# One part of a float64-to-float32 weight conversion: an activation on ScalarE in place of a shift on VectorE

## The chip, the cores and the metric

The kernel runs on one core of a Trainium2 chip. A core has a matrix engine (TensorE, PE in the profile, with its weight loads as PEld), VectorE (DVE), ScalarE (ACT), GpSimd (POOL), and SyncE (SP), which here issues most of the transfers. Each engine works through its own queue in order and waits for the others only through semaphores. The metric is the device time of one execution in microseconds (us); lower is better.

## The reference

Three layers follow one another. All inputs are made in float32 or float64; the weights reach the kernel as float64.

```python
# attention, batch 8, heads 8, 576 positions, head width 64, 32 packing rows p
p_packed = softmax(p @ k.T / 8) @ v          # per head
x = softmax(q @ p_packed.T / 8) @ p_packed   # -> 4608 tokens x 512
# first layer
h = ((x @ w1) * (x @ w2)) @ w3               # 512 -> 1024 -> 1024
x = h @ w_out                                # 1024 -> 512
# second layer, h -> 0 below -1, h above 1, (h + 1)**2 / 4 between
g = gate(x @ w_in)                           # 512 -> 2048
out = g @ w_out2                             # 2048 -> 512
```

## The kernel before

The weights are float64 in memory, eight bytes a value, and the engines work on four. `as_float32` (lines 113 to 138) turns a raw tile of 128 x 512 float64 values into float32 by bits. It views a value as four 16-bit quarters (quarter 0 the lowest). `scale` (L124, ScalarE) reads the upper 32 bits as a float, multiplies by 2^-112 and writes the tile `cvt`. `parts` writes two halves of the output: L129 (VectorE) takes quarter 1 shifted right by 13 bits, so its top three bits, into the low half, and L131 (VectorE) takes the sign bit of quarter 3 into the high half. `join` (L135, VectorE) shifts `cvt` left by three bits and ORs it into the output. There are 72 such conversions.

Forty of them are in the first stage. `ORDER` is a written list of 40 raw tiles: 'o' is a tile of the first layer's w_out (its float32 tile is called `wo`), '3' one of w3 (`w3f`), '12' one of w1 or w2 (`w`). The loop at line 534 goes through this list. In step i it emits the matrix work of `STEPS[i]`, then `convert_begin(i + 1)` (L124 of the next tile), then `convert_end(i)`: L129 and L131 of tile i, L135 of tile i-1, and the load of tile i+4 into the raw buffer that tile i frees (`RAW` is 4 buffers, L110, issued by SP). Only then come the vector and scalar parts of the attention steps. The matrix engine uses the tiles in two ways: L494 multiplies w3 by w_out, one step of four products for each '3' tile, and L192 multiplies w1 and w2 by the packed attention rows.

The other 32 conversions prepare the second layer's weights. `weight_tasks` (line 584) makes eight groups of 18 small tasks, and the loop at line 703 puts one task behind each unit of the first layer's work for batches 1 to 6. Four tasks of a group are conversions (`convert`, L610), into tiles named `cvx`; the others split or combine them (`hl`, L633 on ScalarE and L634 on VectorE) and store them (L641, issued from ScalarE's queue). Here one conversion has its three functions called in a row, there is one `cvt` buffer, and three raw buffers. Between the tasks stand the units: `ab_unit` (products L386, then L396 on ScalarE and L398 on VectorE, then a split L103/L104), `x2_unit` (products L410, then L437 on ScalarE and a store), and the attention of the next batch, with its two exponentials (L215 and L300), its maximum (L208), its score transposes (L294) and its packed rows `pp` (L265).

From about 515 us on the second layer runs without conversions.

Of the kernel before, what the change touches and what calls it, by code (L numbers as in the profile page):

```python
# [13 lines left out]
AF = mybir.ActivationFunctionType  # L14
ALU = mybir.AluOpType
# [40 lines left out]
def fused_kernel(ctx: ExitStack, tc, qT, kT, vv, pb, w1, w2, w3T, wo, win, wout, out):  # L56
    nc = tc.nc
# [55 lines left out]
    def as_float32(pool, raw, out, bufs=1):  # L113

        if raw.dtype == F32:
            return lambda: None, lambda: None, lambda: nc.vector.tensor_copy(out=out, in_=raw)
        quarters = raw.bitcast(U16).rearrange("p (n four) -> p n four", four=4)
        t = pool.tile([P, 512], F32, name="cvt", tag="cvt", bufs=bufs)  # L120
        halves = out.bitcast(U16).rearrange("p (n two) -> p n two", two=2)

        def scale():
            nc.scalar.activation(  # L124
                out=t, in_=raw.bitcast(F32).rearrange("p (n two) -> p n two", two=2)[:, :, 1],
                func=AF.Copy, scale=2.0 ** -112)

        def parts():
            nc.vector.tensor_scalar(  # L129
                out=halves[:, :, 0], in0=quarters[:, :, 1], scalar1=13, scalar2=None, op0=ALU.logical_shift_right)  # L130
            nc.vector.tensor_scalar(  # L131
                out=halves[:, :, 1], in0=quarters[:, :, 3], scalar1=0x8000, scalar2=None, op0=ALU.bitwise_and)

        def join():
            nc.vector.scalar_tensor_tensor(  # L135
                out=out.bitcast(I32), in0=t.bitcast(I32), scalar=3, in1=out.bitcast(I32),
                op0=ALU.logical_shift_left, op1=ALU.bitwise_or)
        return scale, parts, join
# [1035 lines left out]
```

## Time and profile before

| | |
|---|---|
| device time, median of 3 runs | 1330.1 us (1329.04 to 1331.21) |
| profiled execution, its own time | 1334.05 us |
| its span in the profile | 1332.1 us |
| PE busy | 1270.8 us (95% of the span) |
| DVE busy | 879.0 us (66%), 1462 instructions |
| ACT busy | 678.3 us (51%), 1144 instructions |
| L124 on ScalarE | 72 instructions |
| L129 on VectorE | 72 instructions in four groups (32, 16, 16 and 8) |

All durations are from the one profiled execution. Busy time is a union of intervals on an engine, so an idle gap on PE is time in which it had nothing to run. A row of a timeline gives the start, the duration, the engine, the line and operation, and in brackets the idle time just before and who ended it. A duration reaches from start to end; instructions of one engine overlap a little, so the distance between two starts is shorter than a duration. Idle time of an engine that nothing waits for costs nothing.

### The profile page before, as it was taken

How to read it: one execution, taken by the hardware profiler on the slowest of the kernel's cores; microseconds unless marked ns; L12 is line 12 of the kernel's file. 1: busy time of each engine (PE TensorE's matmuls, PEld its weight loads, DVE VectorE, ACT ScalarE, POOL GpSimd, SP SyncE). 2: the span in 40 equal slices, each digit the busy share in tenths (PEclk: the TensorE clock that was granted, in tenths of full speed). 3: DMA queues.
4: the chain of work that ended last, by engine and by line, in shares of the span. 5: the costliest groups of instructions: out<-in, count | busy, mean ns of one | idle time of the engine just before them, and what ended most of it. 6: DMA issues, size and time to landing. Idle time of an engine off the chain costs nothing.

```text
span 1332.1 us, 21124 instructions
## 1 busy us (share of the span) xinstructions
PE 1270.8 (95%) x8184; PEld 1061.1 (80%) x8184; DVE 879.0 (66%) x1462; ACT 678.3 (51%) x1144; POOL 0.7 (0%) x6
## 2 busy tenths in 40 slices
PE   6989889999999999999999999998899899999998
PEld 2367778889888989998777877787878688888888
DVE  5874777778677779635787877877555546455464
ACT  4444354545444555535667766766554343434433
POOL 0000000000000000000000000000000000000000
PEclk9999999999999999999999999999999999999999
DMA  9771575547375543358667675766999967768665
GB/s 362 238 243 59 194 223 180 199 175 273 133 244 155 218 178 125 134 215 299 233 218 270 213 283 199 250 224 205 320 373 375 366 223 266 249 230 290 212 221 176
DMA packets 121299, 307.82 MB, mean 231 GB/s; under 512 B 10352, under 2 KB 45168, under 8 KB 116720
## 3 DMA queue, kind: packets, MB, share of 16 engines
q1 hardware_dynamic: 84304, 237.14, 50.8%
q10 hardware_dynamic: 36896, 69.35, 15.1%
q8 instruction: 64, 1.05, 0.3%
q14 instruction: 35, 0.29, 0.1%
HBM read 200.41 MB, written 106.04 MB: 230 GB/s over the span
## 4 chain that ended last, share of the span: by engine, by line
PE 62%; DMA 15%; DVE 13%; ACT 6%; issue 3%; ACTq 1%; SPq 0%; DVEq 0%
PE x L1090 13%; PE psk L410 13%; PE psk L386 10%; DMA g<-L 7%; PE x L810 7%; PE z L1090 7%; PE y L1090 4%; PE z L810 3%; DMA wi<-hl 2%; PE y L810 2%; PE psk L192 1%; DVE x2s L681 1%; DVE L L874 1%; DMA raw<-w3T 1%; ACT r L818 1%
## 5 line engine op out<-in xcount | busy, mean ns | idle before, releaser
L386 PE MATMUL psk<-at,m 128*128 128x288 f32 x1494 | 215.6, 300 | 4.1 <-DVE at L327 1.9
L386 PEld LDWEIGHTS psk<-at,m 128*128 128x128 f32 x1494 | 201.9, 189 | 18.7 <-issue 11.7
L410 PEld LDWEIGHTS psk<-g,w 128*128 128x128 f32 x1500 | 200.1, 189 | 18.8 <-ACT st L437 7.8
L410 PE MATMUL psk<-g,w 128*128 128x288 f32 x1500 | 206.4, 297 | 4.8 <-ACT st L437 3.3
L810 PE MATMUL x<-x2s,wi 128*128 128x512 f32 (+1 forms) x720 | 163.0, 370 | 3.0 <-ACT m L881 3.0
L956 DVE TENSOR_TENSOR op<-raw,op 128x1024 fp32r<-128x1024 f32 (+1 forms) x94 | 101.7, 1114 | 78.5 <-ACT op L955 78.3
L810 PEld LDWEIGHTS x<-x2s,wi 128*128 128x128 f32 x720 | 126.1, 188 | 28.2 <-ACT m L881 4.5
L955 ACT ACTIVATE op<-raw 128x1024 fp32r<-128x1024 f32 (+1 forms) x94 | 87.3, 967 | 86.0 <-DVE raw L947 38.1
L1090 PE MATMUL x<-op,w 128*128 128x512 f32 (+1 forms) x480 | 103.6, 374 | 4.9 <-DVE op L956 3.2
L1090 PEld LDWEIGHTS x<-op,w 128*128 128x128 f32 x480 | 84.7, 191 | 23.0 <-DVE op L956 5.0
L1090 PE MATMUL x<-op,hwi 128*128 128x512 f32 (+1 forms) x480 | 100.4, 368 | 0.0
L1090 PEld LDWEIGHTS x<-op,hwi 128*128 128x128 f32 x480 | 83.1, 188 | 15.8
L398 DVE TENSOR_TENSOR tb<-psk,ta 128x288 f32<-128x288 f32 x124 | 56.3, 454 | 37.1 <-ACT ta L396 19.5
L821 ACT ACTIVATE r<-r 128x1024 f32<-128x1024 f32 (+1 forms) x80 | 78.0, 975 | 2.5
L956 DVE TENSOR_TENSOR op<-r,op 128x1024 fp32r<-128x1024 f32 (+1 forms) x46 | 50.2, 1118 | 43.5 <-ACT op L955 43.4
L494 PE MATMUL psk<-wo,w3f 128*128 128x512 f32 x128 | 61.4, 631 | 11.9 <-DVE w3f L135 11.9
L634 DVE TENSOR_TENSOR hl<-cvx,hl 128x512 fp32r<-128x512 f32 x56 | 38.4, 686 | 47.0 <-ACT hl L633 44.5
L810 PE MATMUL x<-x2s,ws 128*128 128x512 f32 (+1 forms) x240 | 59.6, 382 | 10.2 <-DVE L L885 9.1
L124 ACT ACTIVATE cvt<-raw 128x512 f32<-128x512 f32 x72 | 48.3, 676 | 40.0 <-DMA raw<-w3T 9.8
L881 ACT ACTIVATE m<-x 128x512 f32<-128x512 f32 (+1 forms) x40 | 22.1, 552 | 90.2 <-PE x L810 81.2
L955 ACT ACTIVATE op<-r 128x1024 fp32r<-128x1024 f32 (+1 forms) x46 | 43.2, 970 | 41.7 <-DVE r L947 14.9
L396 ACT ACTIVATE ta<-psk 128x288 f32<-128x288 f32 x125 | 50.2, 402 | 25.6 <-PE psk L386 21.2
(111 smaller groups left out, 1899.5 us busy)
## 6 DMA issues: line engine op xcount, KB each, us to landing
raw<-g SPq DMA_DIRECT2D x86, 512.0 KB, 5.0
g<-L SPq DMA_DIRECT2D x32, 1024.0 KB, 6.5
r<-g SPq DMA_DIRECT2D x42, 512.0 KB, 5.4
ws<-ws ACTq DMA_DIRECT2D x38, 512.0 KB, 4.9
g<-U SPq DMA_DIRECT2D x64, 256.0 KB, 6.3
w<-hl ACTq DMA_DIRECT2D x28, 512.0 KB, 3.1
x2d<-st ACTq DMA_DIRECT2D x72, 144.0 KB, 2.3
v<-vv SPq DMA_DIRECT2D x8, 1280.0 KB, 7.5
```

Source lines behind the costliest of these rows:

```text
L124: nc.scalar.activation(out=t, in_=raw.bitcast(F32).rearrange("p (n two) -> p n two", two=2)[:, :, 1], func=AF.Copy, scale=2.0 ** -112)
L386: nc.tensor.matmul(ps[w][:, :HS], m_tile[b, w, n][:, s, G, c0 * P:(c0 + 1) * P], at_tile[b][:, G, v, hf * HS:(hf + 1) * HS], start=(k == 0 ...
L396: nc.scalar.activation(out=bs, in_=ps[1][:, :HS], func=AF.Copy)
L398: nc.vector.tensor_tensor(out=g, in0=ps[0][:, :HS], in1=bs, op=ALU.mult)
L410: nc.tensor.matmul(ps, w34[kt][:, s, mt * P:(mt + 1) * P], g_t[kt, hf][:, v, :], start=(kt == kts[0] and n == 0), stop=(kt == kts[-1] and ...
L494: nc.tensor.matmul(acc[4 * hf + m], w3f[hf, j][:, m * P:(m + 1) * P], wof[j], start=(j == 0), stop=(j == 7))
L634: nc.vector.tensor_tensor(out=lo, in0=q[a], in1=hi.bitcast(F32), op=ALU.subtract)
L810: nc.tensor.matmul(bank[s, b][:, :N], w, x2_t[t, q][:, m, k, :N], start=(j == 0 and q in (A11, S1, A12)), stop=(j == 5), skip_group_check= ...
L821: nc.scalar.activation(out=r, in_=r, func=AF.Square)
L955: nc.scalar.activation(out=o[:, :, 0, :N], in_=a[0], func=AF.Copy)
L956: nc.vector.tensor_tensor(out=o[:, :, 1, :N], in0=a[0], in1=o[:, :, 0, :N].bitcast(F32), op=ALU.subtract)
L1090: nc.tensor.matmul(bank[b][d][:, :N], w2_t[q][j // 2][:, 2 * (j % 2) + k, s, d * P:(d + 1) * P], op[x][:, k, v, :N], start=start and k == ...
```

## The change

The low half of the output, the top three bits of quarter 1, is made by ScalarE: the 16-bit integer is multiplied by 2^-13, 4095.5/8192 is taken off, and the result is rounded to a 16-bit integer, which gives the same whole number as the shift. The VectorE shift goes away. It stands in the same place in the program, so it falls into ScalarE's queue there.

```diff
         def parts():
-            nc.vector.tensor_scalar(
-                out=halves[:, :, 0], in0=quarters[:, :, 1], scalar1=13, scalar2=None, op0=ALU.logical_shift_right)
+            nc.scalar.activation(
+                out=halves[:, :, 0], in_=quarters[:, :, 1], func=AF.Copy, scale=2.0 ** -13, bias=-4095.5 / 8192)
             nc.vector.tensor_scalar(
                 out=halves[:, :, 1], in0=quarters[:, :, 3], scalar1=0x8000, scalar2=None, op0=ALU.bitwise_and)
```

In the first stage the ScalarE queue before begins with the scalings of seven tiles one after another, up to the first exponential (`raw` is the float64 tile, `cvt` the scaled one):

```order
L124 ACT_TABLE_LOAD
L124 ACTIVATE cvt<-raw 128x512 x7
L215 ACTIVATE big,sum<-psm,nb 128x576
L124 ACTIVATE cvt<-raw 128x512 x2
L215 ACTIVATE big,sum<-psm,nb 128x576
```

The same place now:

```order
L124 ACT_TABLE_LOAD
L124 ACTIVATE cvt<-raw 128x512 x2
L129 ACTIVATE wo_140<-raw 128x512
L124 ACTIVATE cvt<-raw 128x512
L129 ACTIVATE w3f<-raw 128x512
L124 ACTIVATE cvt<-raw 128x512
L129 ACTIVATE wo_150<-raw 128x512
L124 ACTIVATE cvt<-raw 128x512
L129 ACTIVATE wo_158<-raw 128x512
L124 ACTIVATE cvt<-raw 128x512
L129 ACTIVATE wo_174<-raw 128x512
```

The low half of tile i (the first L129 is that of tile 0) stands behind the scaling of tile i+1, which waits for tile i+1 to be loaded.

In the first group of the second layer's weights, VectorE's queue before, around the second conversion (`mx` and `nb` feed the exponential, `tb` and `g` are the first layer's):

```order
L208 TENSOR_REDUCE mx<-psm 128x1
L210 TENSOR_SCALAR nb<-mx 128x1
L129 TENSOR_SCALAR cvx<-raw 128x512
L131 TENSOR_SCALAR cvx<-raw 128x512
L135 SCALAR_TENSOR_TENSOR cvx<-cvt,cvx 128x512
L398 TENSOR_TENSOR tb<-psk_1626,ta 128x288
```

ScalarE's queue now, at the third conversion of the same group, with the exponential ahead of it and `ta`, which L398 needs, behind it:

```order
L215 ACTIVATE big,sum<-psm,nb 128x576
L124 ACTIVATE cvt<-raw 128x512
L129 ACTIVATE cvx<-raw 128x512
L396 ACTIVATE ta<-psk_1685 128x288
L103 ACTIVATE g_1663<-tb 128x288
```

VectorE loses the row L129 there and the rest keeps its order; ScalarE has one instruction more between the scaling and `ta`.

## Rows read from the trace of the kernel before

**Rows 1.** The page's first part: engine, busy us (share of span), instructions.
```profile
PE 1270.8 (95%) x8184; PEld 1061.1 (80%) x8184; DVE 879.0 (66%) x1462; ACT 678.3 (51%) x1144; POOL 0.7 (0%) x6
```

**Rows 2.** Stretches: length, busy PE, PEld, DVE, ACT, POOL, clock, DMA share, GB/s.
```profile
45.00:77.00 32.00, 27.42 (x110) 11.35 (x108) 30.33 (x62) 15.28 (x27) 0.00 (x0) 1.00 0.64 221
164.00:200.00 36.00, 30.98 (x307) 27.59 (x304) 25.95 (x60) 19.25 (x47) 0.00 (x0) 0.95 0.69 213
200.00:515.00 315.00, 307.98 (x2900) 275.96 (x2899) 234.72 (x486) 160.14 (x363) 0.00 (x0) 1.00 0.55 192
```

**Rows 3.** Groups by line and shape: busy us, mean ns of one, idle before.
```profile
L124 ACT ACTIVATE cvt<-raw 128x512 f32<-128x512 f32 x72 | 48.3, 676 | 40.0 <-DMA raw<-w3T 9.8 <-DMA raw<-wo 8.5 <-DMA raw<-w 8.2
...
L633 ACT ACTIVATE hl<-cvx 128x512 fp32r<-128x512 f32 x56 | 35.3, 630 | 32.8 <-DMA wi<-hl 12.7 <-DVE cvx L135 7.4 <-ACT st L437 5.2
...
L955 ACT ACTIVATE op<-raw 128x1024 fp32r<-128x1024 f32 x75 | 76.2, 1054 | 75.2 <-DVE raw L947 33.8 <-DVE L L1067 25.7 <-DMA raw<-g 10.4
...
L881 ACT ACTIVATE m<-z 128x512 f32<-128x512 f32 x32 | 18.5, 579 | 0.8 <-PE z L810 0.8
...
L129 DVE TENSOR_SCALAR cvx<-raw 128x512 uint16<-128x512 uint16 x32 | 14.7, 458 | 0.0
```

**Rows 4.** Timeline of PE, first 100 us, where it sat idle.
```profile
18.01 1.19 PE L181 MATMUL psm<-qk,pb 128*64 128x288 f32 x8 [2.44 <-ACT big L215]
...
46.49 7.33 PE L494 MATMUL psk<-wo,w3f 128*128 128x512 f32 x16 [1.48 <-DVE w3f L135]
...
59.27 1.13 PE L494 MATMUL psk<-wo,w3f 128*128 128x512 f32 x2 [1.19 <-DVE w3f L135]
...
74.39 1.60 PE L386 MATMUL psk<-at,m 128*128 128x288 f32 x9 [1.50 <-DVE m L104]
...
97.22 2.89 PE L386 MATMUL psm<-at,m 128*128 128x288 f32 x12 [4.00 <-ACT st L437]
```

**Rows 5.** Timeline of ACT and DVE in the first 30 us.
```profile
26.36 1.26 ACT L124 ACTIVATE cvt<-raw 128x512 f32<-128x512 f32 x2
...
13.87 0.44 DVE L131 TENSOR_SCALAR wo<-raw 128x512 uint16<-128x512 uint16 x1
14.20 0.68 DVE L135 SCALAR_TENSOR_TENSOR wo<-cvt,wo 128x512 int32<-128x512 int32 x1
14.80 0.47 DVE L129 TENSOR_SCALAR w3f<-raw 128x512 uint16<-128x512 uint16 x1
15.15 0.46 DVE L131 TENSOR_SCALAR w3f<-raw 128x512 uint16<-128x512 uint16 x1
```

**Rows 6.** Raw tiles: load times of L110 to 115 us, then when tiles are taken up.
```profile
DMA to landing us min/median/max: 3.5/5.3/10.2
...
36.83 0.68 ACT L124 ACTIVATE cvt<-raw 128x512 f32<-128x512 f32 x1 [0.89 <-DMA raw<-w]
...
45.07 0.47 DVE L129 TENSOR_SCALAR w3f<-raw 128x512 uint16<-128x512 uint16 x1 [1.07 <-DMA raw<-w3T]
...
45.13 0.69 ACT L124 ACTIVATE cvt<-raw 128x512 f32<-128x512 f32 x1 [1.75 <-DMA raw<-w3T]
```

**Rows 7.** Waits of the whole run: us in total, times, longest.
```profile
DVE cvx L135 <- ACT cvt L124: 12.4, 10, 2.1
```

**Rows 8.** Timeline of ACT, DVE and PE, 366 to 389 us, rows that wait.
```profile
367.10 0.66 ACT L124 ACTIVATE cvt<-raw 128x512 f32<-128x512 f32 x1
...
367.79 0.69 DVE L135 SCALAR_TENSOR_TENSOR cvx<-cvt,cvx 128x512 int32<-128x512 int32 x1 [0.80 <-ACT cvt L124]
...
375.34 0.63 ACT L633 ACTIVATE hl<-cvx 128x512 fp32r<-128x512 f32 x1 [2.11 <-DMA wi<-hl]
...
379.02 0.34 PE L274 MATMUL psm<-ident,pp 128*128 128x128 f32 x1 [0.52 <-DVE pp L265]
...
388.61 0.72 PE L192 MATMUL psm<-qk,ppt 64*32 64x288 f32 x16 [2.02 <-DVE big L294]
```

**Rows 9.** Timeline of PE and DVE at two other groups of conversions.
```profile
277.16 0.69 DVE L135 SCALAR_TENSOR_TENSOR cvx<-cvt,cvx 128x512 int32<-128x512 int32 x1
278.87 1.32 PE L410 MATMUL psk<-g,w 128*128 128x288 f32 x8 [1.36 <-ACT st L437]
...
409.85 3.44 PE L410 MATMUL psk<-g,w 128*128 128x288 f32 x24 [0.51 <-ACT st L437]
```

## The prediction

> **What bounds the kernel now.** The page's first part comes first: the matrix engine is busy for 1270.8 of 1332.1 us [rows 1], so all that any change elsewhere can win is the 61.3 us in which it sits idle. VectorE is at 66% and ScalarE at 51%: moving work between them wins nothing by the averages. Next the stretches. The conversions stand before 116 us (40 of them) and between 164 and 510 us (32). Between 45 and 77 us VectorE is busy for 30.33 of 32 us and the matrix engine idles for 4.58 [rows 2]: there the change takes work from the busiest engine. Between 164 and 200 us the matrix engine idles for 5.02 us, and over the following 315 us for only 7.02 [rows 2]. So I read third the timeline of the matrix engine, gap by gap [rows 4, 9], and for each gap what stands in the other two queues ahead of its releaser. After 515 us nothing is touched.
>
> **What an operation costs.** Removed: 72 shifts of 0.458 us [rows 3]. The next VectorE instruction starts 0.35 us after a shift starts (14.80 to 15.15), and the sign part L131 holds its engine for 0.33 (13.87 to 14.20) [rows 5], so VectorE gets 72 x 0.35 = 25 us back, 14 of it in the first stage. Added: 72 activations on ScalarE that no row shows, with 16-bit data, read at a stride of eight bytes. The nearest row is the scaling L124, which reads the same raw tile at the same stride: 0.676 us. A contiguous one, L633, takes 0.630, one that reads the matrix engine's banks 0.579, and one of twice the elements 1.054 [rows 3]. I take 0.68 from start to end and 0.60 for a place in the queue (two scalings end 1.26 us after the first starts, [rows 5]); the bounds are 0.58 and 1.05. That is 72 x 0.60 = 43 us more in ScalarE's queue.
>
> The Trainium skill (ScalarE: Activation LUTs, What ACT_TABLE_LOAD costs) gives an activation with immediate scale and bias 186 ns plus 0.833 ns an element: 613 ns by that estimate for 512. The strided row says 676, so the measured one stands. By the page each wait below would be some 0.06 us shorter, and the sum about 0.3 us lower.
>
> **How the waiting changes.** Before, both parts were VectorE's own, and L135 needed only the scaling from ScalarE. Now L135 of a tile also needs ScalarE's L129. Where VectorE is behind and ScalarE ahead, the conversion is 0.35 us shorter. Where both start together, on a landed tile or behind an exponential, L135 came after 0.35 + 0.33 = 0.68 us of shifts; now it comes after 0.60 of scaling, 0.68 of L129 and about 0.05 of signalling, 1.33, so 0.65 later. Whatever is queued behind either waits too: on VectorE L398, the maxima and the splits, on ScalarE `ta`, `st` and the exponentials.
>
> **First stage, step by step.** Until 18.01 us the loads pace everything. The exponential that the matrix engine waits for at 18.01 [rows 4] stands behind an L135 that comes 0.65 later: +0.65. The matrix engine is then busy to 45.0 us and waits 1.48 us for the L135 of the w3 tile that follows the landing at 45.07 [rows 4, 6]. That L135 was ready to start 0.69 us after the landing and is 0.65 later now, which replaces the earlier shift and does not add to it. The landing moves also. A raw buffer was free 0.8 us after its tile landed (0.35 and L131's 0.45). Now L129 of tile i is queued behind the scaling of tile i+1, so the buffer waits for the next tile plus 1.3 us, and the next load in SP's queue with it. Against that stands that the loads up to 33 us are limited by the key, value and query loads between them. Following the queue through by hand, load by load, I get tile 20 late by between 0 and 1.9 us; I take 0.9, so the gap at 46.49 ends 1.5 us later. Between 46.5 and 74.4 us VectorE is never idle for more than a moment, and ten conversions stand on it: 10 x 0.35 = 3.5 us less. Three of the ten L135 find ScalarE late (behind the exponential of the second scores, behind the split L326, behind a late tile) and give about 1.9 back. Net -1.6: the resumption at 74.39 comes at +1.5 - 1.6 = -0.1, so nothing. The 4.00 us before 97.22 [rows 4] hang on a store of x2 that lands among the loads of the next keys and values, and no conversion decides it: 0. First stage: 0, at best -2.7 (the gaps at 59.27 and 74.39 gone), at worst +3.4 (1.9 late by landings, 0.65 by L135, and 0.9 more of the gap at 74.39).
>
> **The second layer's weights, group by group.** Of the 32 L135 there, ten already wait for ScalarE, 12.4 us in all [rows 7]; each of those gets 0.6 later. There are eight groups of four. The group at 357 to 370 us shows it: the third scaling starts at 367.10 behind the exponential, L135 waits 0.80 for it and starts at 367.79 [rows 8]. The second conversion is 0.6 late in the same way and pushes the exponential, so the third starts 1.2 later. The split L633 at 375.34 waits for a store that was issued right behind that exponential [rows 8], so it is late by some 0.6, and so are the two gaps of the matrix engine at 379.02 and 388.61, which hang on it: +0.8. The same pattern in the first group, where the matrix engine has less lead (5.02 us idle, [rows 2]): +1.0. The groups before 278.87 and its twin 192 us later go the other way: there VectorE is late and L135 at 277.16 waits for nobody [rows 9]; it comes 0.6 earlier and the 1.36 us gap shrinks by 0.55, twice -0.55. The `st` at 409.85 stands behind a scaling and now also behind L129 [rows 9]: +0.6, and +0.2 at its twin, where the matrix engine has a lead. The two groups at 308 and 500 us show no gap: 0. Sum: 1.0 + 0.8 - 1.1 + 0.8 = +1.5 us. The bounds are -2.7 (both gaps of the kind at 278.87 gone) and +6 (all ten waits, 0.6 each, reach the matrix engine).
>
> **The sum.** 0 + 1.5 = +1.5 us on the profiled execution of 1334.05 us (span 1332.1 and 1.95 around it). That execution took 3.95 us more than the median of the runs; the difference carries over, so 1330.1 + 1.5 = 1331.6 us.
>
> **Rivals.**
> First, the raw buffers become the bound (slower). Before, a cycle of four buffers is (0.8 + 5.3) / 4 = 1.5 us a tile by the median landing [rows 6]; now one buffer is always held, (1.3 + 5.3) / 3 = 2.2. Tiles came every 2.08 us (36.83 to 45.13, four tiles, [rows 6]). It decides from a landing of 3 x 2.08 - 1.3 = 4.9 us on. Price: 0.12 us a tile, 4.6 over 38 tiles, less the 1.50 gap at 74.39, plus the 1.5 of the second part: +4.6, 1334.7 us. For it speaks that the median lies above 4.9, against it the shortest landing of 3.5, and that 5.3 was measured with four in flight.
>
> Second, relief wins (faster). If ScalarE always has L129 done before VectorE gets there, the gaps at 59.27 and 74.39 go (2.7 us), the two like 278.87 (2.7), and nothing is lost: -5.4, 1324.7 us. For it speaks ScalarE's 15.28 busy us out of 32 where VectorE is full [rows 2]; against it that two of the four early gaps end with a landing or a store, and the ten waits of [rows 7].
>
> Third, the 16-bit activation is slow, at the upper bound of 1.05 us. Each L135 that waits is 0.4 later again, about five of them with the matrix engine behind (+1.9) and two in the first stage (+0.8): 1334.3 us. The stride alone speaks against it, since L124 has it too.
>
> A rule of the Trainium skill (ScalarE: Activation LUTs, Rules for kernel authors) speaks against the change as such: additions and multiplications belong on VectorE. The rows agree as far as they go, 0.676 against 0.458; the first and third rival say what it would cost.
>
> **How the numbers follow.** About 0.2%, 2.7 us, is what a measurement of this kernel tells from no change. My forecast has a chance of 0.50, and its own range is 1328.5 to 1334: 0.44 within 0.2%, 0.05 slower, 0.01 faster. The buffers have 0.25 (0.22 slower, 0.03 within), relief 0.18 (0.16 faster, 0.02 within), the slow activation 0.07 (0.06 slower, 0.01 within). So faster 0.17, the same 0.50, slower 0.33. The range of 1326 to 1336 reaches most of the way to the rivals on both sides, and their worst ends are left out.
>
> **What the profile would show.** Right: 72 L129 on ScalarE near 0.68 us; VectorE's busy time down by some 25 us and ScalarE's up by some 43; L135 waiting for ScalarE in most groups; the gap at 46.49 longer, that at 59.27 nearly gone; the gaps at 379.02 and 388.61 longer. The raw buffers as a bound would show as SP's L110 waiting for ScalarE and as tiles landing ever later up to 90 us. Wrong I would be if the matrix engine reached 77 us more than 2 us earlier or later than before, or if the stretch from 164 to 515 us changed by more than 3 us.

## The result, and the profile after

| | before | after |
|---|---|---|
| device time, median of 4 runs each on one chip | 1329.65 us (1329.04 to 1331.21) | 1343.33 us (1343.05 to 1344.07) |
| ratio to before, 95% interval | | 1.0103 (1.0084 to 1.0122) |
| profiled execution: own time, span | 1334.05, 1332.1 us | 1343.42, 1341.6 us |
| second comparison, median of 4 runs (before: of 8) | 1330.6 us | 1339.71 us, 1.0068 (1.0053 to 1.0083) |

The change makes the kernel slower, by 0.7 to 1.0%. The forecast was 1331.6 us, in a range of 1326 to 1336.

The page's first part of the changed kernel (engine, busy us, share, instructions) answers to [rows 1]:

```profile
PE 1278.1 (95%) x8184; PEld 1065.5 (79%) x8184; DVE 857.3 (64%) x1390; ACT 721.3 (54%) x1216; POOL 0.7 (0%) x6
```

The work moved as forecast: VectorE has 21.7 us less to do (25 said), ScalarE 43.0 us more (43 said). The loss therefore has to be looked for in the waits. Where, the matrix engine's timeline of the changed kernel shows (start us, duration, operation, in brackets the idle time before and who ended it). It answers to [rows 4, 8, 9]:

```profile
38.48 3.70 PE L494 MATMUL psk<-wo,w3f 128*128 128x512 f32 x8 [1.16 <-DVE w3f L135]
46.01 6.62 PE L494 MATMUL psk<-wo,w3f 128*128 128x512 f32 x8 [3.72 <-DVE w3f L135]
53.73 7.43 PE L494 MATMUL psk<-wo,w3f 128*128 128x512 f32 x16 [0.45 <-DVE w3f L135]
66.12 10.57 PE L494 MATMUL psk<-wo,w3f 128*128 128x512 f32 x24 [0.45 <-DVE w3f L135]
80.65 1.59 PE L386 MATMUL psk<-at,m 128*128 128x288 f32 x9 [1.13 <-DVE m L104]
103.32 3.25 PE L386 MATMUL psm<-at,m 128*128 128x288 f32 x12 [2.53 <-ACT st L437]
...
284.46 6.62 PE L410 MATMUL psk<-g,w 128*128 128x288 f32 x48 [0.43 <-ACT st L437]
385.96 0.33 PE L274 MATMUL psm<-ident,pp 128*128 128x128 f32 x1 [0.85 <-DVE pp L265]
394.91 0.72 PE L192 MATMUL psm<-qk,ppt 64*32 64x288 f32 x16 [1.38 <-DVE big L294]
415.99 3.44 PE L410 MATMUL psk<-g,w 128*128 128x288 f32 x24 [0.35 <-ACT st L437]
```

The step of 16 products that began at 46.49 [rows 4] begins at 53.73, 7.2 us late. The resumption at 74.39 comes at 80.65 (+6.3), the one at 97.22 at 103.32 (+6.1), the step behind the `st` at 409.85 [rows 9] at 415.99 (+6.1). So the first stage loses 7.2 us before 54 us. The steady +6 behind it hides two things, though. Just ahead of the second layer's weights there is this step, first before, then in the changed kernel:

```profile
160.07 3.52 PE L386 MATMUL psk<-at,m 128*128 128x288 f32 x23 [1.93 <-DVE at L327]
```

```profile
163.61 3.52 PE L386 MATMUL psk<-at,m 128*128 128x288 f32 x23 [0.78 <-DVE at L327]
```

Here the changed kernel is only 3.5 us late: about half of the loss has been won back, mostly in places where the matrix engine waited anyway. The stretch with the conversions of the second layer's weights, up to 515 us, then adds 2.6 us (6.2 us late at its end). Both parts of the change cost time.

What the matrix engine waits for in the first stage is a tile that comes late. ScalarE's timeline of the changed kernel, the tiles near 45 us; it answers to [rows 6]:

```profile
35.05 0.69 ACT L124 ACTIVATE cvt<-raw 128x512 f32<-128x512 f32 x1 [2.51 <-DMA raw<-w3T]
...
43.90 0.67 ACT L124 ACTIVATE cvt<-raw 128x512 f32<-128x512 f32 x1 [1.85 <-DMA raw<-w]
44.47 0.76 ACT L129 ACTIVATE w3f<-raw 128x512 uint16<-128x512 uint16 x1
...
49.37 0.66 ACT L124 ACTIVATE cvt<-raw 128x512 f32<-128x512 f32 x1 [1.52 <-DMA raw<-w3T]
49.93 0.76 ACT L129 ACTIVATE wo<-raw 128x512 uint16<-128x512 uint16 x1
51.61 0.67 ACT L124 ACTIVATE cvt<-raw 128x512 f32<-128x512 f32 x1 [0.91 <-DMA raw<-w3T]
```

Tile 16, taken up at 36.83 before, is taken up at 43.90; tile 20 at 51.61 instead of 45.13, 6.5 us late. Each of these scalings waits for a transfer. The transfers are no slower: the load times of the same stretch stand beside those of [rows 6].

```profile
DMA to landing us min/median/max: 3.4/5.2/9.4
```

They are issued later. What SP's queue waited for in the first 130 us (us in total, times, longest), the two longest waits of L110 before, then those of the changed kernel:

```profile
SPq L110 <- DVE w3f L131: 26.6, 13, 4.3
...
SPq L110 <- DVE w L131: 26.0, 14, 4.3
```

```profile
SPq L110 <- DVE w L131: 19.8, 10, 4.1
SPq L110 <- ACT w3f L129: 16.5, 11, 2.7
SPq L110 <- ACT wo L129: 15.8, 7, 4.0
...
SPq L110 <- ACT w L129: 6.7, 6, 3.7
```

Before, the waits of L110 were for VectorE, all but 4.5 us of them. Now 39 us are waits for the new activation L129, which is then the last reader of a raw buffer and so the one that frees it. L110 waits for little longer in all (68 us before, 75 now); what changed is whom it waits for. How that hold comes about shows at the load of tile 7, where the two engines' rows of the changed kernel fit together, ScalarE first, then SP:

```profile
13.65 0.68 ACT L124 ACTIVATE cvt<-raw 128x512 f32<-128x512 f32 x1 [3.08 <-DMA raw<-wo]
14.23 0.76 ACT L129 ACTIVATE wo<-raw 128x512 uint16<-128x512 uint16 x1
...
15.02 2.91 SPq L110 DMA_DIRECT2D raw<-w3T  x3
```

The L129 at 14.23 belongs to tile 3. It stands behind the scaling of tile 4, which waits until 13.65 for its own data. When it ends, at 14.99, the load of tile 7 goes out at 15.02. Before, that load went out at 9.95.

### The profile page after: what moved, and what is told of

Read it like the earlier page. It is cut to its first block, busy times and chain, and to the rows that moved or that the text cites. A ratio compares the mean times of both kernels' runs of the same rounds, so it can differ in the third digit from the quotient of the medians.

```text
span 1341.6 us, 21129 instructions
## 1 busy us (share of the span) xinstructions
PE 1278.1 (95%) x8184; PEld 1065.5 (79%) x8184; DVE 857.3 (64%) x1390; ACT 721.3 (54%) x1216; POOL 0.7 (0%) x6
## 4 chain that ended last, share of the span: by engine, by line
PE 65%; DMA 13%; DVE 11%; ACT 7%; issue 2%; ACTq 1%; SPq 0%; DVEq 0%
PE x L1090 13%; PE psk L410 11%; PE psk L386 10%; PE x L810 9%; PE z L1090 6%; DMA g<-L 5%; PE z L810 4%; PE y L1090 4%; PE y L810 2%; DMA raw<-w3T 2%; PE psk L192 1%; DMA wi<-hl 1%; DVE x2s L681 1%; DMA r<-g 1%; ACT cvt L124 1%
## 5 line engine op out<-in xcount | busy, mean ns | idle before, releaser
L398 DVE TENSOR_TENSOR tb<-psk,ta 128x288 f32<-128x288 f32 x124 | 56.1, 452 | 37.2 <-ACT ta L396 19.1
L124 ACT ACTIVATE cvt<-raw 128x512 f32<-128x512 f32 x72 | 48.6, 674 | 35.2 <-DMA raw<-w3T 10.5
L494 PEld LDWEIGHTS psk<-wo,w3f 128*128 128x128 f32 x128 | 25.4, 207 | 48.6 <-issue 27.9
```

The costliest lines, as they stand in the source:

```text
L124: nc.scalar.activation(out=t, in_=raw.bitcast(F32).rearrange("p (n two) -> p n two", two=2)[:, :, 1], func=AF.Copy, scale=2.0 ** -112)
L398: nc.vector.tensor_tensor(out=g, in0=ps[0][:, :HS], in1=bs, op=ALU.mult)
L494: nc.tensor.matmul(acc[4 * hf + m], w3f[hf, j][:, m * P:(m + 1) * P], wof[j], start=(j == 0), stop=(j == 7))
```

## The experiments

The theories were: the raw buffers, held until the next tile has landed, bound the first stage (the first rival); or the tiles are made late because L135 waits for ScalarE, or the sheer 0.77 us an activation costs. Each ratio below, with its 95% interval, is to the kernel before on the same chip. Lines behind an inserted edit have numbers that are up to 6 higher.

**One half of the change at a time.** The first kernel has the activation in the first stage only, the second in the second layer's weights only (there the condition reads `!=`):

```diff
+            if bufs == CVT:
+                nc.scalar.activation(
+                    out=halves[:, :, 0], in_=quarters[:, :, 1], func=AF.Copy, scale=2.0 ** -13, bias=-4095.5 / 8192)
+            else:
                 nc.vector.tensor_scalar(
                     out=halves[:, :, 0], in0=quarters[:, :, 1], scalar1=13, scalar2=None, op0=ALU.logical_shift_right)
```

> The 40 conversions of the first stage have their low half on ScalarE, the 32 of the second layer's weights keep the shift on VectorE. Theory (held buffers: in the first stage the low half of a tile is queued behind the scaling of the next tile, which waits for its load, so raw buffers come free late, tiles land late and the matrix engine idles and then runs at half clock): 8 to 13 us slower than before, 1338 to 1343 us. Rival (length: the activation takes 0.77 us and every conversion loses alike, 40 of 72 of the loss): 6 to 8 us slower, 1336 to 1338 us. Rival (the second layer's weights lose it): under 4 us slower.

> The other half: the first stage keeps the shift on VectorE, the 32 conversions of the second layer's weights have the low half on ScalarE. Held buffers: 0 to 4 us slower than before, 1330 to 1334 us, and the first 116 us as before. Length: 5 to 7 us slower, 1335 to 1337 us. The second layer's weights lose it: 9 us slower or more.

Measured: 1.0032 (1.0012 to 1.0052) for the first stage, 3.1 us where held buffers were expected to cost 8 to 13 (under 4 was what the weights as the main loss would have meant); 1.0026 (1.0002 to 1.0049) for the weights, 2.9 us and within the 0 to 4 expected. So the two halves cost about the same, and the first stage is only about half of the loss. Together that is 0.58%; both at once gave 0.68% and 1.03% in two comparisons, so the halves add up within the interval of the 0.68% and leave some 0.45% of the other open. In the first of these kernels tile 20 is taken up at 50.49, 5.4 us late, so the lateness in the first stage is there without the other half. In the weights no buffer is held for the next tile, since a conversion's three functions stand in a row; between 160 and 520 us SP's L110 waits for L129 for 2.8 us in all in the changed kernel. What cost time there was not taken away by itself in any run.

**The same instructions, in another place of ScalarE's queue.** The activation moves from `parts` into `scale`, right behind the scaling of its own tile. So it no longer waits for the next tile to land:

```diff
                 func=AF.Copy, scale=2.0 ** -112)
+            nc.scalar.activation(
+                out=halves[:, :, 0], in_=quarters[:, :, 1], func=AF.Copy, scale=2.0 ** -13, bias=-4095.5 / 8192)
```

> All 72 low halves on ScalarE as in the changed kernel, but each stands right behind the scaling of its own tile, so in the first stage it no longer waits for the next tile. Same instructions on both engines, same durations. Held buffers: the first stage's loss goes, 0 to 4 us slower than before, 1330 to 1334 us, SP no longer waits for L129 for longer than about a microsecond, tile 20 lands within 1 us of before. Length: as the changed kernel, 1341 to 1344 us.

Measured: 1.0012 (0.9997 to 1.0026). All 72 activations are still there, and most of the loss is gone, as held buffers would have it. Tile 20 is taken up at 44.91 (45.13 before). In the weights this kernel has the order of the changed one, so the difference comes from the first stage.

**The hold without the conversion, and the conversion's cost without the hold.** Both kernels keep the shift on VectorE and add one more activation of the same size to each of the 40 first-stage tiles, in the same place of the queue; it writes a tile that nothing reads. In the first it reads the raw tile, so it holds the buffer; in the second it reads a constant tile, so it holds nothing:

```diff
+            if bufs == CVT:
+                s = pool.tile([P, 512], U16, name="spare", tag="spare", bufs=1)
+                nc.scalar.activation(
+                    out=s, in_=quarters[:, :, 1], func=AF.Copy, scale=2.0 ** -13, bias=-4095.5 / 8192)
```

> The kernel before with an activation more in the first stage: the same as that of the change, in the same place of ScalarE's queue, reading the same raw tile, but written into a spare tile that nobody reads. The shift stays on VectorE. So ScalarE is as busy and the raw buffer is held until the next tile is scaled, but L135 waits for nothing new. Held buffers: 3 to 7 us slower than before, and the loads come as late as with the change. Lateness of L135: under 2 us slower, since only the chain through L135 would cost.

> The kernel with the unused extra activation in the first stage again (shift on VectorE, result read by nobody), but it reads a constant tile of the same shape and stride in place of the raw tile. ScalarE is as busy in the same places, and no raw buffer is held by it. Held buffers: 0 to 2 us slower than before, and tile 20 lands as early as before. If it is ScalarE's queue itself that is too full: 6 to 9 us slower, like the one that holds the buffer (1.0068).

Measured: with the hold 1.0068 (1.0051 to 1.0084), 9.3 us where 3 to 7 were expected; without it 1.0015 (0.9996 to 1.0034). The two take the same time on ScalarE (666 and 669 ns a piece). The hold alone thus costs more than the change of the first stage, which has the same hold and came to 1.0032. That one also spares VectorE 40 shifts, which the difference puts at some 0.36%; the two intervals just touch, so the size is uncertain. What SP waited for in the kernel with the hold, in the first 130 us, and its issues of the loads:

```profile
SPq L110 <- ACT spare L133: 37.5, 21, 4.1
```

```profile
15.01 2.87 SPq L110 DMA_DIRECT2D raw<-w3T  x3
20.01 0.33 SPq L110 DMA_DIRECT2D raw<-wo  x1
23.43 0.33 SPq L110 DMA_DIRECT2D raw<-w  x1
...
36.50 0.33 SPq L110 DMA_DIRECT2D raw<-w3T  x1
```

The same issues in the changed kernel, behind the one at 15.02 shown above:

```profile
20.18 0.33 SPq L110 DMA_DIRECT2D raw<-wo  x1
23.70 0.33 SPq L110 DMA_DIRECT2D raw<-w  x1
...
36.44 0.33 SPq L110 DMA_DIRECT2D raw<-w3T  x1
```

And before, where these four went out at 9.95, 17.81, 19.07 and 27.64:

```profile
9.95 6.04 SPq L110 DMA_DIRECT2D raw<-w3T  x3
17.81 0.33 SPq L110 DMA_DIRECT2D raw<-wo  x1
...
19.07 0.33 SPq L110 DMA_DIRECT2D raw<-w  x1
...
27.64 0.33 SPq L110 DMA_DIRECT2D raw<-w3T  x1
```

An extra reader that changes no arithmetic gives, to 0.3 us, the schedule of loads of the changed kernel. In the kernel without the hold SP's longest wait for the extra activation is 0.4 us, tile 20 is taken up at 44.37, and the matrix engine's resumption at 74.39 stays at 74.38.

**More raw buffers.** The changed kernel, the one with the other place in the queue, and the kernel before, each with six:

```diff
-RAW, CVT, W3, VPOS = 4, 6, 4, 6
+RAW, CVT, W3, VPOS = 6, 6, 4, 6
```

> The changed kernel with six raw buffers in the first stage in place of four. A buffer is still held until the next tile's scaling, but loads are issued two tiles earlier. Held buffers, if the late issue of loads is the larger part: 3 to 8 us less than the changed kernel, 1335 to 1340 us, with tile 20 landing as early as before. If the lateness of L135 by itself is the larger part (the wait behind the next tile's scaling, 0.7 to 1 us at each step that the matrix engine waits for): under 2 us less, 1341 to 1343 us. Length: no difference.

> All low halves on ScalarE, each right behind the scaling of its own tile, and six raw buffers. Held buffers: with six buffers the order matters little any more, 0 to 2 us from the changed kernel with six buffers (1325.95). Lateness of L135: the own order is then worth 2 to 5 us more, 1321 to 1324 us.

> The kernel before (shift on VectorE everywhere) with six raw buffers in the first stage in place of four. If the held buffer was what the change cost there and nothing more is to be had from early loads: 0 to 2 us less than before. If early loads help the kernel before as well: 3 to 8 us less, 1324 to 1329 us, and the changed kernel with six buffers (1325.95) owes its time to the buffers and not to ScalarE.

> The kernel before with seven raw buffers. If a buffer held longer is all that is at stake, six are enough and this is within 1 us of six (0.9946). If the first stage is still short of loads with six: 1 to 3 us less.

Measured: the changed kernel 0.9961 (0.9945 to 0.9977), with the other place 0.9948 (0.9929 to 0.9967), the kernel before 0.9946 (0.9931 to 0.9961) and, with seven buffers, 0.9963 (0.9945 to 0.998). Two more buffers take 1.1% off the changed kernel (1.0068 to 0.9961), more than the 3 to 8 us expected, and 0.5% off the kernel before. So four buffers already cost the kernel before something, and the change made that worse; with six, the changed kernel and the kernel before can't be told apart for certain. A seventh brings nothing more.

The changed kernel was also timed a second time, beside the kernel with the hold.

> The changed kernel itself, once more beside the others, because the two halves of the change taken one at a time came to 1.0032 and 1.0026 times before and the whole to 1.0103 in the first measurement. If the losses add up: 1.006, 7 to 9 us slower than before. If the whole is more than its halves (late tiles meet late weights, or the matrix engine's clock falls more often): 1.009 to 1.012 again, 12 to 15 us.

Measured: 1.0068 (1.0053 to 1.0083), near the 1.006 that was expected if the halves add up. That the hold alone has the same ratio is chance: the whole change has VectorE's relief (some -0.36%) and the cost of the weights (0.26%) besides. At the step that begins at 849.47 us before, this profile is 4.1 us late and the first one of the changed kernel 4.4 (853.52 and 853.86). They part only behind it, where nothing was changed and conversions no longer run: the remaining time is 483.8 us here, 487.7 in the first profile and 482.6 before, with half the clock granted for 13.6, 17.0 and 10.2 us of it. Of the 3.9 us by which the two profiles part there, 2.3 arise between the steps that begin at 1050 and 1100 us before, where the first has half the clock for 6.8 us from 1058.9 and the second for 3.4 from 1058.0. What decides that part stays open, and with it the difference of the two ratios. It also means that the end of a single profile says little: that of the kernel with the first stage alone is on time at 849.47 and ends 2.2 us late.

**The best of both.** Activation in the first stage only, right behind its own scaling, the shift kept for the second layer's weights, six raw buffers:

```diff
-RAW, CVT, W3, VPOS = 4, 6, 4, 6
+RAW, CVT, W3, VPOS = 6, 6, 4, 6
...
                 func=AF.Copy, scale=2.0 ** -112)
+            if bufs == CVT:
+                nc.scalar.activation(
+                    out=halves[:, :, 0], in_=quarters[:, :, 1], func=AF.Copy, scale=2.0 ** -13, bias=-4095.5 / 8192)
...
-            nc.vector.tensor_scalar(
-                out=halves[:, :, 0], in0=quarters[:, :, 1], scalar1=13, scalar2=None, op0=ALU.logical_shift_right)
+            if bufs != CVT:
+                nc.vector.tensor_scalar(
+                    out=halves[:, :, 0], in0=quarters[:, :, 1], scalar1=13, scalar2=None, op0=ALU.logical_shift_right)
```

> What the runs so far point to: six raw buffers, the 40 low halves of the first stage on ScalarE right behind the scaling of their own tile, the 32 of the second layer's weights on VectorE. If the halves add up (second layer's weights on ScalarE cost 1.0026): 2 to 4 us less than all on ScalarE with six buffers (0.9948), so 0.992 to 0.993 of before, 1320 to 1321 us. If VectorE's relief in the first stage is worth nothing once loads come early: as the kernel before with six buffers, 0.9946.

Measured: 1318.05 us, 0.9895 (0.9869 to 0.9922), more than was expected, and faster than both kernels and than six buffers alone. This profile is its fastest execution, 1314.38 us. Its matrix engine, in the rows that answer to [rows 4]:

```profile
49.42 1.98 PE L498 MATMUL psk<-wo,w3f 128*128 128x512 f32 x4 [0.19 <-DVE w L104]
52.24 3.67 PE L498 MATMUL psk<-wo,w3f 128*128 128x512 f32 x8 [0.19 <-DVE w3f L139]
56.36 10.57 PE L498 MATMUL psk<-wo,w3f 128*128 128x512 f32 x24 [0.45 <-DVE w3f L139]
69.44 1.59 PE L390 MATMUL psk<-at,m 128*128 128x288 f32 x9 [0.64 <-DVE m L104]
...
88.75 1.87 PE L390 MATMUL psm<-at,m 128*128 128x288 f32 x12 [0.48 <-ACT st L441]
```

The gap of 1.48 at 46.49 is gone, 1.19 and 1.50 have become 0.45 and 0.64, and the wait of 4.00 us before 97.22 is down to 0.48. Before 69 us VectorE's relief counts once the tiles are there: with six buffers alone the resumption of 74.39 comes at 71.61, here at 69.44. With six buffers alone:

```profile
71.61 1.59 PE L386 MATMUL psk<-at,m 128*128 128x288 f32 x9 [1.50 <-DVE m L104]
```

## Why the prediction was wrong, point by point

**The step that failed** is this one: "Following the queue through by hand, load by load, I get tile 20 late by between 0 and 1.9 us; I take 0.9". Measured: 6.5 us. The mechanism stood two sentences before it (a raw buffer is held until the next tile has landed and 1.3 us more), and its rate stood in the first rival, which had a chance of 0.25. Tile 8 is taken up here, before and in the changed kernel:

```profile
19.19 0.67 ACT L124 ACTIVATE cvt<-raw 128x512 f32<-128x512 f32 x1 [0.67 <-DMA raw<-w3T]
```

```profile
22.32 0.69 ACT L124 ACTIVATE cvt<-raw 128x512 f32<-128x512 f32 x1 [2.16 <-DMA raw<-w3T]
```

So 3.1 of the 6.5 us are there by tile 8. The other 3.4 come by the rate: from tile 8 to tile 20 the kernel before goes from 19.19 to 45.13, 2.16 us a tile, the changed one from 22.32 to 51.61, 2.44. The rival had 2.2 for a ring of three, with loads of 5.3 us. Three times 2.44 is 7.3; by that estimate, if the ring paced all of these tiles, the cycle of a buffer was 1.3 us of hold and 6.0 for the issue, the load and the turn on ScalarE, not 5.3. Behind tile 20 the ring no longer decides: up to tile 32 both kernels need about 2.6 us a tile. The rival's formula decided from a landing of 4.9 us on and the median was 5.3: it said yes, and the hand count, which gave no, was believed instead. The loads of key, value and query, which were to cover for it up to 33 us, did not: the load of tile 7, in their midst, goes out 5.1 us late, that of tile 15 8.8 (36.44 for 27.64).

**The relief that was to bring it back.** "Between 46.5 and 74.4 us VectorE is never idle for more than a moment", so 3.5 us were to be won there and the resumption at 74.39 to be on time. It was 6.3 us late. The stretches of the changed kernel (length, busy PE, PEld, DVE, ACT, POOL, clock, DMA share, GB/s) answer to [rows 2]:

```profile
45.00:77.00 32.00, 29.86 (x92) 11.83 (x96) 25.32 (x48) 22.13 (x38) 0.00 (x0) 0.89 0.67 216
...
164.00:200.00 36.00, 30.64 (x302) 26.98 (x300) 23.42 (x54) 19.86 (x47) 0.00 (x0) 1.00 0.73 230
200.00:515.00 315.00, 306.96 (x2872) 274.35 (x2873) 224.72 (x454) 175.68 (x389) 0.00 (x0) 0.99 0.55 193
```

Between 45 and 77 us VectorE is busy for 25.32 us instead of 30.33, but 6 to 7 us late this is not the same work. From the same step to the same resumption it is, first before, then in the changed kernel:

```profile
46.49:74.39 27.90, 25.22 (x96) 9.71 (x96) 26.97 (x56) 13.17 (x22) 0.00 (x0) 1.00 0.63 217
```

```profile
53.73:80.65 26.92, 25.11 (x97) 9.64 (x97) 23.79 (x46) 19.03 (x32) 0.00 (x0) 1.00 0.63 202
```

VectorE has 3.2 us less to do, near the 3.5 said, and the stretch is 1.0 us shorter, by the smaller gaps (1.19 to 0.45, 1.50 to 1.13). The rest became idle time of VectorE (0.9 us before, 3.1 now), 2.8 us of it in waits for ScalarE, which is busy for 5.9 us more here. An engine that is freed while its input comes later gains idle time.

**The new wait of L135** was sized about right in the first stage: 0.65 us each was said, and with 0.95 at the exponential of 18.01 (18.96 now) the first step nearly holds. It was low in the weights. The waits of the whole changed kernel, beside [rows 7]:

```profile
DVE cvx L135 <- ACT cvx L129: 24.8, 18, 3.5
```

Instead of 12.4 us in 10 waits and 0.6 more for each, it is 24.8 us in 18. Yet the second layer's weights stayed within what was said: +1.5 with bounds of -2.7 and +6. Measured alone they cost 0.26%, 3.5 us (0.3 to 6.5 by the interval); at 515 us that kernel's profile is 1.8 us late, and in the changed kernel's the stretch from 164 to 515 us is 2.6 longer, inside the 3 us that the prediction gave as its limit. Its other limit, 2 us at 77 us, was passed: +6.3 at the resumption of 74.39. By pieces, in the profile of the weights alone: the matrix engine is 1.5 us late behind the first group (197.45, 1.0 said), the 1.36 us gap before 278.87 shrank to 0.45 as told, and the one at 379.02 grew from 0.52 to 1.16. But the one at 388.61 did not grow, it shrank from 2.02 to 0.90, so that a lateness of 2.9 us was back at 1.8; and the gap at 409.85 grew by 0.1 and not by 0.6.

**The price of the operation** was low: 0.68 us taken. The shapes of L129 in the changed kernel, by line (busy us, mean ns of one, idle before):

```profile
L129 ACT ACTIVATE cvx<-raw 128x512 uint16<-128x512 uint16 x32 | 25.1, 786 | 0.0
...
L129 ACT ACTIVATE w3f<-raw 128x512 uint16<-128x512 uint16 x16 | 12.3, 767 | 0.4 <-ACT st L437 0.4
```

The 0.1 us between does not carry the result: the kernel without the hold has 40 activations of 0.67 us and stays within 0.2%, and the one with each activation behind its own scaling has all 72 at the full price for 0.12%. By the estimate from the Trainium skill (ScalarE: Activation LUTs, What ACT_TABLE_LOAD costs) it would have been 613 ns; the rows say 767 to 786, and the trace does not agree. The page states its figures for fp32 and bf16, not for 16-bit integers.

**What had no term.** The matrix engine's clock. The step at 46.01 takes 6.62 us for the eight products that took 3.70 at 38.48: the granted clock stands at half, 1.2 in place of 2.4 GHz, from 45.1 to 51.9, which makes the 0.89 of the stretch above (6.8 of 32 us at half); it fell in the 3.72 us in which the engine had nothing to run. There it is mostly hidden, since the next step waits for its tile anyway (0.45 us before 53.73). Over the run without its last 3 us, the changed kernel has 34.1 us at half clock and the kernel before 20.5; at half speed these 13.6 us more cost 6.8 where nothing hides them. Half of the 13.6 lie behind 849 us, in code that was not changed.

**The rivals.** The buffers were the cause of the first stage's loss: without the hold most of the loss is gone (1.0012), and the hold alone makes one (1.0068). Their price, 0.12 us a tile over 38 tiles, was 0.28 over the twelve from tile 8, with 3.1 us already there, and the time of 1334.7 was 8.6 us short of the median. They are not the cause in the weights, where L135's longer waits are the likely one; that is argued from the waits and not shown by a run. Relief as the main effect fell. The slow activation fell as the main cause. The rule of the Trainium skill that additions and multiplications belong on VectorE (ScalarE: Activation LUTs, Rules for kernel authors) is half borne out: in the weights the activation costs 0.26%, or 0.5% with six buffers and its own place (0.9948 with it, 0.9895 without), but in the first stage, with these, it takes the kernel from 0.9946 to 0.9895.

## What to carry to other kernels

Before moving the last reader of a buffer to another engine's queue, look at what stands directly ahead of it there: where that is the first reader of the next buffer, a ring of n is a ring of n-1, and n is no longer what the code says. Work out the ring's rate from the loads' median, add what the issue and the reader's turn take, and believe it over a hand count that has other transfers cover the difference. Relief of a busy engine is worth something only when its input isn't made later by the same edit; place the new instruction behind its own tile's first reader, give the ring more buffers, and here the relief pays (0.9946 to 0.9895).

## What the runs showed of the hardware that was not expected

The activation's time depends on how it writes. With 16-bit input at a stride of eight bytes in both cases, the one into every second 16-bit word takes 767 to 786 ns, the one into a contiguous tile 666 ns (the extra activation with the hold, 40 times):

```profile
L133 ACT ACTIVATE spare<-raw 128x512 uint16<-128x512 uint16 x40 | 26.6, 666 | 0.4 <-ACT st L441 0.4
```

Reading a raw tile or a constant one makes no difference (666 and 669). VectorE's own work does not explain it: with VectorE idle meanwhile L129 takes 770 ns in the changed kernel on average, with VectorE busy 783. The scaling L124, which was taken as the nearest row, also writes without gaps, and that is where the 0.68 came from.
